# Attention inside a fused layer: products with v for eight key chunks at a time instead of four, and the four score tiles of such a phase issued one by one

## The chip, the cores and the metric

One core of a Trainium2 chip runs the whole program in one launch. The metric is the device time of one execution in microseconds (us); several executions are timed and the median is quoted. TensorE (PE) multiplies, VectorE (DVE) and ScalarE (ACT) work on its results in PSUM, GpSimd (POOL) works in SBUF, SyncE (SP) issues the transfers. "PEld" is TensorE's loading of weights.

## The reference

Three layers follow one another: attention with 32 heads (4 batches of 8), a gated MLP and a channel MLP. Only the first is touched by the change.

```python
q_pool = q.reshape(B, H, S // factor, factor, D).mean(axis=3)        # S 1152 -> 576
scores = scale * np.matmul(q_pool, k.transpose(0, 1, 3, 2))          # 576 x 1152 a head
scores = scores - np.max(scores, axis=-1, keepdims=True)
attn = np.exp(scores)
attn = attn / (np.sum(attn, axis=-1, keepdims=True) + 1e-09)
return np.matmul(attn, v).astype(np.float32)                         # D = 64
```

## The kernel before

Two heads that lie on partitions 0 to 63 and 64 to 127 are worked on together, so `NP` = 16 pairs `j`. A pair's 576 queries are cut in three jobs `u` of `N` = 192, and the 1152 keys in `KC` = 9 chunks of 128: 48 x 9 = 432 units `(u, c)`. The main loop takes them in 108 groups of `G` = 4; a group is two score tiles of two units each. The program is written in the order in which each engine runs it (no scheduler moves anything), so the text of the loop is the order in every engine's queue.

Four kinds of TensorE work alternate in the loop:

- **Scores** (`scores`, L245) and the subtraction of the maximum (`less`, L261 and L264): contraction over 64 rows, two heads side by side in the array. The rows of the trace say 64\*128. ACT then takes the exponential of the whole tile (`expo`, L268) into an SBUF tile `pt` (8 of them), and POOL adds the tiles of a job up for the softmax sum (L282, L285).
- **Pieces** (`piece`): the maxima of the scores are needed before the scores themselves, so rounded copies of q and k are multiplied ahead of time, for a later pair, piece by piece: mostly two matmuls of 512 columns in the 64\*128 form (L161, reduced by DVE at L180), some of 128 columns (L161 with L188, reduced at L191 and after), and 16 in all that use the full array (`c == 2`, L175, rows 128\*128, reduced at L176). `some()` issues one as long as the piece count is behind `end`.
- **Products with v** (`pv`, L292), and the sums over the keys (`sums`, L307): contraction over 128 rows, 64 columns of output a head. The rows say 128\*64. `sums` runs once a job, and ACT copies its result (L311).
- **Transposes** (`to_rows`, L219 and L226), once a pair: they turn the maxima into rows, which ACT copies into `toprow` (L229, L236); `less` needs that.

Score tiles, pieces and transposes share one PSUM ring, the pool `ps_s` with the tag "s" and three slots. The fourth tile to be issued waits until the first one has been read, by ACT if it was a score tile and by DVE if it was a piece.

One group is issued as: a piece; both score tiles; both subtractions and exponentials; a piece; then `pv` for the group before. `also(i)` closes it: it advances the second layer's weight loading by one tick (`Weights.tick`). From group 8 on a unit of weights is begun at every fourth tick, at groups 8, 12, 16 and so on, with two ACT steps in the first tick (L547, L548; the five units of the spatial weights skip them), and one more (L568) six ticks later; DVE steps (L552, L554, L558) lie at ticks one, two and five. In the groups 3 and 4 of a pair, `round_k` (L143) and `round_q` (L132, L137) round the next-but-one pair's k and q on ACT.

Of the kernel before, what the change touches and what calls it, by code (L numbers as in the profile page):

```python
# [31 lines left out]
def attention(tc, idf, q, k, v, xs, rounded, also):  # L32
# [31 lines left out]
    with ExitStack() as ctx, ExitStack() as sco:  # L64
# [84 lines left out]

        pieces = []  # L150
        for u in range(2 * NP):
            for c in range(2):
                pieces += [(u, c, PW * i) for i in range(NPC)]
            pieces += [(u, 2, None)] * (u % 2) + [(u, None, NPC * PW)]
        upto = [sum(x[0] < u for x in pieces) for u in range(2 * NP + 1)]
        done = [0]

# [2 lines left out]
            p = slice(D * e, D * e + D)  # L160
            nc.tensor.matmul(o, s["qr"][p, q0:q0 + 128], s["kr"][p, k0:k0 + n], start=True, stop=True)  # L161

        def piece(r=None):
            u, c, k0 = pieces[done[0]]
            done[0] += 1
            s, jb = st[u // 2], halves[u]
            r = ring("r") if r is None else r
            if "m" not in jb:
                jb["m"] = ld.tile([128, 2, 2, NPC + 1], F32, tag="m", name="m", bufs=4)
                if u % 2:  # L170
                    jb["md"] = ld.tile([128, 2], F32, tag="md", name="md", bufs=2)
            m = jb["m"]
            if c == 2:
                for h in range(NPC):
                    nc.tensor.matmul(r[:, h], s["qd"], s["kr"][:, PW * h:PW * h + PW], start=True, stop=True)  # L175
                nc.vector.tensor_reduce(out=jb["md"][:, 0:1], in_=r, axis=AX.XY, op=ALU.max, negate=True)  # L176
            elif c is not None:
                for e in range(2):
                    rounded_scores(r[:, e], u, c, e, k0, PW)
                nc.vector.tensor_reduce(out=m[:, c, :, k0 // PW], in_=r, axis=AX.X, op=ALU.max, negate=True)  # L180
            else:
                for c in range(2):
                    for e in range(2):
                        rounded_scores(r[:, e, REST * c:REST * c + REST], u, c, e, k0, REST)
                if u % 2:
                    for e in range(2):
                        p = slice(D * e, D * e + D)
                        nc.tensor.matmul(  # L188
                            r[:, e, 2 * REST:3 * REST], s["qd"][p], s["kr"][p, k0:S], start=True, stop=True
                        )  # L190
                nc.vector.tensor_reduce(  # L191
                    out=m[:, :, :, NPC].rearrange("p c e -> p e c"),
                    in_=r[:, :, 0:2 * REST].rearrange("p e (c x) -> p e c x", c=2),
                    axis=AX.X, op=ALU.max, negate=True,
                )
                t = tops[u // 2 % 2]
                if u % 2:
                    for e in range(2):
                        p = slice(D * e, D * e + D)
                        nc.vector.tensor_reduce(  # L200
                            out=jb["md"][p, 1:2], in_=r[p, e, 2 * REST:3 * REST], axis=AX.X, op=ALU.max, negate=True
                        )
                        nc.vector.tensor_reduce(out=t[p, 4, e, 0:1], in_=jb["md"][p], axis=AX.X, op=ALU.min)
                nc.vector.tensor_reduce(
                    out=t[:, 2 * (u % 2):2 * (u % 2) + 2, :, 0], in_=m, axis=AX.X, op=ALU.min
                )
# [31 lines left out]
        def scores(pair):  # L238

            t = ps_s.tile([128, 2, 512], F32, tag="s", name="s")  # L240
            for x, (u, c) in enumerate(pair):
                s, q0 = st[u // 3], N * (u % 3)
                for e in range(2):
                    p = slice(D * e, D * e + D)
                    nc.tensor.matmul(  # L245
                        t[:, e, N * x:N * x + N], s["k"][p, 128 * c:128 * c + 128], s["q"][p, q0:q0 + N],
                        start=x == 0, stop=False,
                    )
            return t
# [37 lines left out]
        def pv(u, c):  # L287
            jb = jobs[u]
            if c == 0:
                jb["o"] = ps_o.tile([128, 512], F32, tag="o", name="po")  # L290
            for e in range(2):
                nc.tensor.matmul(  # L292
                    jb["o"][D * e:D * e + D, 0:N], st[u // 3]["v"][:, e, c], jb["p", c][:, e],
                    start=c == 0, stop=c == KC - 1,
                )

        def sums(u):

            jb = jobs[u]
            terms = [jb["acc"][:, :, N * i:N * i + N] for i in range(W)]  # L300
            terms += [jb["p", c] for c in ((KC - 1,) if u % 2 == 0 else ())]
            if u == NJ - 1:
                terms += [jb["p", c] for c in range(KC - 4, KC)]
            r = jb["o"][:, 256:256 + N]
            for i, x in enumerate(terms):
                for e in range(2):
                    nc.tensor.matmul(  # L307
                        r[D * e:D * e + D], ones, x[:, e], start=i == 0, stop=i == len(terms) - 1
                    )
            t = jb["sum"] = ld2.tile([128, N], F32, tag="sum", name="sum")  # L310
            nc.scalar.activation(t, r, ACTF.Copy, bias=1e-9)  # L311

        def recip(u, i):
            t = jobs[u]["sum"][:, N * i // 2:N * (i + 1) // 2]
            nc.vector.reciprocal(out=t, in_=t)  # L315

        def out(u):
            jb = jobs[u]
            q0 = N * (u % 3)
            x = ld2.tile([128, N], F32, tag="x", name="x")  # L320
            nc.vector.tensor_tensor(out=x, in0=jb["o"][:, 0:N], in1=jb["sum"], op=ALU.mult)
            b, h = divmod(u // 3, HP)
            nc.sync.dma_start(out=xs[b][2 * D * h:2 * D * h + 2 * D, q0:q0 + N], in_=x)
# [18 lines left out]
        pool_q(0, nc.gpsimd, 256, T)  # L342
        round_q(0, 256, T)
        for i in range(upto[1]):
            piece()
            busy(4 if i > 1 else 0)
        pool_q(1, nc.gpsimd)
        busy(14)
# [12 lines left out]
        for i, group in enumerate(groups):  # L361
            for u, c in group:
                if c == KC - 1 and u < NJ - 1:
                    sums_at[i + 1] = u
                    for n in range(2):
                        smalls.setdefault((i + 2, n), []).append(lambda u=u, n=n: recip(u, n))
                    smalls.setdefault((i + 3, 0), []).append(lambda u=u: out(u))
        j = 0
        for i, group in enumerate(groups):
            if j + 1 < NP and at[j + 1] == i:  # L370
                j += 1
            r = i - at[j]
            if r == 0:
                if j + 2 < NP:
                    load_k(j + 2)
                    load_q(j + 2)
                if j + 1 < NP:
                    load_v(j + 1)

            end = min(upto[2] + -(-upto[2] * (4 * i + 8) // (3 * KC)), upto[2 * NP])  # L380

            def some(t=None):
                if done[0] < end:
                    piece(t)

            new = []
            if i == 2:
                new = [1]
            elif r == 0 and j:
                new = [2 * j, 2 * j + 1]  # L390
            for u in new:
                while done[0] < upto[u + 1]:
                    piece()
            if new:
                to_rows(*new)
            else:
                some()
            for x in smalls.pop((i, 0), ()):
                x()
            tiles = [group[x:x + W] for x in range(0, G, W)]  # L400
            ts = [scores(pair) for pair in tiles]
            for pair, t in zip(tiles, ts):
                less(pair, t)
                expo(pair, t)
            some()

            for _ in range(2 if i < 4 else 0):
                if done[0] < end:
                    piece()
            for x in smalls.pop((i, 1), ()):  # L410
                x()
            if i + 1 == len(groups):
                break
            for x in before:
                pv(*x)
            before = group

            if i in sums_at:
                sums(sums_at[i])
            also(i)  # L420
            if r == 2 and j + 2 < NP:
                pool_q(j + 2, nc.gpsimd)

            if r == 3 and j + 2 < NP:
                round_k(j + 2)
            if r == 4 and j + 2 < NP:
                round_q(j + 2)
        sco.close()
        for x in before:
            pv(*x)  # L430
        before = group
        for x, names in zip(before, LEFT):
            pv(*x)
# [832 lines left out]
```

## Time and profile before

| what | us |
|---|---|
| three timed executions: lowest, median, highest | 1159.83, 1162.37, 1163.08 |
| the profiled execution | 1156.86 |
| its span in the trace | 1155.1 |
| mean granted TensorE clock in it | 0.995 of full speed |
| busy: PE, PEld | 1124.0 (97%), 963.8 (83%) |
| busy: DVE, POOL, ACT | 581.3 (50%), 517.4 (45%), 441.8 (38%) |

The profiled execution takes 1.8 us beyond its span, and 5.5 us less than the median. A matmul's end in the trace is modelled and it overlaps the next one's start, so a busy PE says little; what counts is the distance from one start to the next. A float32 matmul shows up as two records, and the two heads run side by side, so "x16" on the score line of a group is eight steps: two tiles of four.

### The profile page before, as it was taken

The numbers are of one execution on the slowest core, as the hardware profiler recorded it, in microseconds if no ns is written. First come the engines' busy times: TensorE is split into PE (matmuls) and PEld (weight loads), VectorE is DVE, ScalarE is ACT, GpSimd is POOL, SyncE is SP. The second block draws the span as 40 slices with busy tenths as digits, with TensorE's granted clock in tenths as the row PEclk, the third lists the DMA queues.
The fourth block names the chain that finished last, engine by engine and source line by source line (L and its number), as shares of the span: only waits on it lengthen the run. The fifth ranks groups of instructions, "written<-read, shape, count | busy, mean of one in ns | idle before, by whom it ended". The sixth has DMA issues, their size and how long they took to land.

```text
span 1155.1 us, 20475 instructions
## 1 busy us (share of the span) xinstructions
PE 1124.0 (97%) x8530; PEld 963.8 (83%) x8530; DVE 581.3 (50%) x882; ACT 441.8 (38%) x822; POOL 517.4 (45%) x400
## 2 busy tenths in 40 slices
PE   7999999999999999999999998999999999999998
PEld 6777777888878888788988997789989999999997
DVE  5667777766778766244242427788722121121211
ACT  3455554555555554443333325455411111111110
POOL 3578786877777776524242427575600000000000
PEclk9999999999999999999999998999999999999999
DMA  6143422333524321011111016244302010010000
GB/s 164 45 122 92 122 79 77 83 99 86 129 76 130 83 73 35 9 57 46 42 42 51 1 51 228 78 146 131 116 1 82 1 35 21 1 55 1 28 1 28
DMA packets 40079, 79.32 MB, mean 69 GB/s; under 512 B 5809, under 2 KB 20145, under 8 KB 39986
## 3 DMA queue, kind: packets, MB, share of 16 engines
q1 hardware_dynamic: 39986, 78.01, 23.0%
q8 instruction: 67, 1.10, 0.4%
q14 instruction: 26, 0.21, 0.1%
HBM read 63.31 MB, written 14.16 MB: 67 GB/s over the span
## 4 chain that ended last, share of the span: by engine, by line
PE 52%; DVE 3%; POOL 1%; ACT 1%; issue 1%; POOLq 0%
PE ph L1114 17%; PE py L1128 17%; PE pu L866 4%; PE pv L731 4%; PE pg L884 4%; PE py L914 3%; DVE st L558 1%; PE pV L939 1%; DVE st L552 1%; PE pt L1106 1%; POOL st L556 1%; PE pU L900 1%; DVE st L554 0%; POOL gt L449 0%; PE po L307 0%
## 5 line engine op out<-in xcount | busy, mean ns | idle before, releaser
L1128 PE MATMUL py<-w,h 128*128 128x512 f32 x864 | 218.4, 397 | 3.0 <-ACT h L1117 2.7
L268 ACT ACTIVATE pt<-s 128x768 f32<-128x768 f32 x216 | 163.3, 808 | 149.8 <-PE s L261 138.8
L1114 PE MATMUL ph<-ut,w 128*128 128x384 f32 x1152 | 218.6, 338 | 0.0
L1114 PEld LDWEIGHTS ph<-ut,w 128*128 128x128 f32 x1152 | 205.7, 188 | 8.5
L180 DVE TENSOR_REDUCE m<-r 128x2 f32<-128x1024 f32 x128 | 155.8, 1223 | 75.4 <-PE r L161 74.9
L282 POOL TENSOR_TENSOR acc<-pt,acc 128x768 f32<-128x768 f32 x94 | 173.4, 1845 | 41.8 <-ACT pt L268 37.4
L1128 PEld LDWEIGHTS py<-w,h 128*128 128x128 f32 x864 | 160.2, 188 | 34.2 <-ACT h L1117 3.3
L1118 DVE SCALAR_TENSOR_TENSOR h<-ph,h 128x384 fp32r<-128x384 f32 x96 | 53.4, 557 | 268.6 <-ACT h L1117 268.6
L292 PE MATMUL po<-pt,v 128*64 128x192 f32 x1728 | 164.5, 332 | 0.0
L245 PE MATMUL s<-q,k 64*128 64x192 f32 x1728 | 163.0, 328 | 1.0 <-ACT pt L268 0.6
L1117 ACT ACTIVATE h<-ph 128x384 fp32r<-128x384 f32 x96 | 47.1, 491 | 304.5 <-PE ph L1114 304.5
L245 PEld LDWEIGHTS s<-q,k 64*128 64x128 f32 x1728 | 142.1, 187 | 11.2 <-issue 4.1
L292 PEld LDWEIGHTS po<-pt,v 128*64 128x64 f32 x1728 | 114.3, 136 | 39.3 <-issue 26.1
L282 POOL TENSOR_TENSOR acc<-pt 128x768 f32<-128x768 f32 x48 | 88.0, 1834 | 83.0 <-ACT pt L268 82.9
L315 DVE RECIPROCAL sum<-sum 128x96 f32<-128x96 f32 x96 | 69.7, 737 | 42.6 <-ACT sum L311 42.6
L161 PE MATMUL r<-yh 64*128 64x512 f32 (+1 forms) x384 | 71.7, 398 | 13.0 <-DVE m L180 7.1
L556 POOL TENSOR_TENSOR st<-st,raw 128x512 int32<-128x512 int32 (+3 forms) x48 | 68.8, 1435 | 19.4 <-issue 11.0
L261 PE MATMUL s<-toprow,yh 64*128 64x384 f32 x416 | 68.2, 401 | 0.0
L161 PEld LDWEIGHTS r<-yh 64*128 64x128 f32 x384 | 34.1, 184 | 40.5 <-issue 12.2
L884 PE MATMUL pg<-wst,vn 128*128 128x288 f32 x448 | 60.1, 295 | 0.0
L884 PEld LDWEIGHTS pg<-wst,vn 128*128 128x128 f32 x448 | 59.6, 188 | 0.0
L866 PEld LDWEIGHTS pu<-xt,wi 128*128 128x128 f32 x384 | 53.3, 188 | 2.1
(125 smaller groups left out, 1291.5 us busy)
## 6 DMA issues: line engine op xcount, KB each, us to landing
raw<-in_moe_w_ch_dram SPq DMA_DIRECT2D x32, 512.0 KB, 3.7
k<-in_k_dram SPq DMA_DIRECT2D x32, 288.0 KB, 4.4
qraw<-in_q_dram SPq DMA_DIRECT2D x32, 288.0 KB, 5.7
v<-in_v_dram SPq DMA_DIRECT2D x16, 576.0 KB, 4.1
x<-x SPq DMA_DIRECT2D x48, 96.0 KB, 1.7
xn<-x SPq DMA_DIRECT2D x4, 1152.0 KB, 5.7
out_dram<-un SPq DMA_DIRECT2D x18, 256.0 KB, 2.1
raw<-in_moe_w_in_dram SPq DMA_DIRECT2D x8, 512.0 KB, 4.3
```

The lines of the kernel that those rows point to most:

```text
L161: nc.tensor.matmul(o, s["qr"][p, q0:q0 + 128], s["kr"][p, k0:k0 + n], start=True, stop=True)
L180: nc.vector.tensor_reduce(out=m[:, c, :, k0 // PW], in_=r, axis=AX.X, op=ALU.max, negate=True)
L245: nc.tensor.matmul(t[:, e, N * x:N * x + N], s["k"][p, 128 * c:128 * c + 128], s["q"][p, q0:q0 + N], start=x == 0, stop=False,)
L268: nc.scalar.activation(x, t[:, :, 0:W * N], ACTF.Exp, scale=SC)
L282: nc.gpsimd.tensor_tensor(out=a, in0=x, in1=jb["t"] if c < 4 else a, op=ALU.add)
L292: nc.tensor.matmul(jb["o"][D * e:D * e + D, 0:N], st[u // 3]["v"][:, e, c], jb["p", c][:, e], start=c == 0, stop=c == KC - 1,)
L315: nc.vector.reciprocal(out=t, in_=t)
L556: nc.gpsimd.tensor_tensor(out=o, in0=o, in1=lo, op=ALU.add)
L866: nc.tensor.matmul(p[:, 0:HT], wi[0][:, a, k, 128 * m:128 * m + 128], xt[:, c, k, HT * h:HT * h + HT], start=i == 0, stop=i == 3 * KD - 1,)
L884: nc.tensor.matmul(p[:, 0:HT], vn[:, a, s, 128 * m:128 * m + 128], wst[:, c, s, sl], start=s == 0 and i == 0, stop=s == NT - 1 and i == 1,)
L1114: nc.tensor.matmul(p[:, 0:BT], w1s[m][:, a, k], ut[i][:, c, k], start=j == 0, stop=j == 3 * KD - 1)
L1128: nc.tensor.matmul(py[i][c], h[:, a, 128 * c:128 * c + 128], w2s[m][:, e], start=m == 0 and a + e == 0, stop=m == KM - 1 and a == 1,)
```

## The change

`pv` and `sums` run in odd groups alone, for the two groups before: 16 matmul instructions instead of 8 (a phase is an even group and the odd one behind it). A score tile's subtraction and exponential follow it at once, before the next tile's scores. Pieces go to the front of the even group, to its end, and to the end of the odd group, where there can be two; full-array pieces are swapped with the next one unless they lie beside the products with v. The sums, reciprocals and outputs of a job move with `pv`. The names "r0" and "r1" take slots of the same ring.

```diff
@@ -149,9 +149,10 @@
 
         pieces = []
         for u in range(2 * NP):
+            pieces += [(u, 2, None)] * (u % 2)
             for c in range(2):
                 pieces += [(u, c, PW * i) for i in range(NPC)]
-            pieces += [(u, 2, None)] * (u % 2) + [(u, None, NPC * PW)]
+            pieces += [(u, None, NPC * PW)]
         upto = [sum(x[0] < u for x in pieces) for u in range(2 * NP + 1)]
         done = [0]
 
@@ -160,8 +161,11 @@
             p = slice(D * e, D * e + D)
             nc.tensor.matmul(o, s["qr"][p, q0:q0 + 128], s["kr"][p, k0:k0 + n], start=True, stop=True)
 
-        def piece(r=None):
-            u, c, k0 = pieces[done[0]]
+        def piece(r=None, beside=True):
+            x = done[0]
+            if not beside and pieces[x][1] == 2 and pieces[x + 1][1] is not None:
+                pieces[x], pieces[x + 1] = pieces[x + 1], pieces[x]
+            u, c, k0 = pieces[x]
             done[0] += 1
             s, jb = st[u // 2], halves[u]
             r = ring("r") if r is None else r
@@ -342,7 +346,7 @@
         pool_q(0, nc.gpsimd, 256, T)
         round_q(0, 256, T)
         for i in range(upto[1]):
-            piece()
+            piece(ps_s.tile([128, 2, 512], F32, tag="s", name="r0") if i % 3 else None)
             busy(4 if i > 1 else 0)
         pool_q(1, nc.gpsimd)
         busy(14)
@@ -361,10 +365,11 @@
         for i, group in enumerate(groups):
             for u, c in group:
                 if c == KC - 1 and u < NJ - 1:
-                    sums_at[i + 1] = u
+                    at_sum = i + 1 + i % 2
+                    sums_at.setdefault(at_sum, []).append(u)
                     for n in range(2):
-                        smalls.setdefault((i + 2, n), []).append(lambda u=u, n=n: recip(u, n))
-                    smalls.setdefault((i + 3, 0), []).append(lambda u=u: out(u))
+                        smalls.setdefault((at_sum + 1, n), []).append(lambda u=u, n=n: recip(u, n))
+                    smalls.setdefault((at_sum + 2, 0), []).append(lambda u=u: out(u))
         j = 0
         for i, group in enumerate(groups):
             if j + 1 < NP and at[j + 1] == i:
@@ -379,9 +384,9 @@
 
             end = min(upto[2] + -(-upto[2] * (4 * i + 8) // (3 * KC)), upto[2 * NP])
 
-            def some(t=None):
-                if done[0] < end:
-                    piece(t)
+            def some(beside=False, lag=0):
+                if done[0] < end - lag:
+                    piece(beside=beside)
 
             new = []
             if i == 2:
@@ -393,30 +398,33 @@
                     piece()
             if new:
                 to_rows(*new)
-            else:
-                some()
+            elif i % 2 == 0:
+                some(True)
             for x in smalls.pop((i, 0), ()):
                 x()
-            tiles = [group[x:x + W] for x in range(0, G, W)]
-            ts = [scores(pair) for pair in tiles]
-            for pair, t in zip(tiles, ts):
+            for x in range(0, G, W):
+                pair = group[x:x + W]
+                t = scores(pair)
                 less(pair, t)
                 expo(pair, t)
-            some()
+            some(bool(i % 2))
+            if i % 2 and i > 3:
+                some(True)
 
             for _ in range(2 if i < 4 else 0):
                 if done[0] < end:
-                    piece()
+                    piece(ps_s.tile([128, 2, 512], F32, tag="s", name="r1"))
             for x in smalls.pop((i, 1), ()):
                 x()
             if i + 1 == len(groups):
                 break
-            for x in before:
-                pv(*x)
-            before = group
-
-            if i in sums_at:
-                sums(sums_at[i])
+            if i % 2:
+                for x in before:
+                    pv(*x)
+                before = []
+                for u in sums_at.pop(i, ()):
+                    sums(u)
+            before = before + group
             also(i)
             if r == 2 and j + 2 < NP:
                 pool_q(j + 2, nc.gpsimd)
@@ -428,6 +436,10 @@
         sco.close()
         for x in before:
             pv(*x)
+        for i in sorted(sums_at):
+            for u in sums_at[i]:
+                if u < NJ - 1:
+                    sums(u)
         before = group
         for x, names in zip(before, LEFT):
             pv(*x)
```

How the engines' rows move. First TensorE in groups 8 and 9: `r` is a piece, `s` a score tile, `po` the output of `pv`. Before:

```order
L161 MATMUL r<-yh 128x128 x4
L245 MATMUL s<-q,k 128x192 x8
L261 MATMUL s<-toprow,yh 128x384 x4
L161 MATMUL r<-yh 128x512 x2
L292 MATMUL po<-pt,v 64x192 x8
L161 MATMUL r<-yh 128x512 x2
L245 MATMUL s<-q,k 128x192 x8
L261 MATMUL s<-toprow,yh 128x384 x4
L292 MATMUL po<-pt,v 64x192 x8
```

The same two groups with the change (the lines are numbered four higher there):

```order
L249 MATMUL s<-q,k 128x192 x4
L265 MATMUL s<-toprow,yh 128x384 x2
L249 MATMUL s<-q,k 128x192 x4
L265 MATMUL s<-toprow,yh 128x384 x2
L162 MATMUL r<-yh 128x128 x4
L249 MATMUL s<-q,k 128x192 x4
L265 MATMUL s<-toprow,yh 128x384 x2
L249 MATMUL s<-q,k 128x192 x4
L265 MATMUL s<-toprow,yh 128x384 x2
L179 MATMUL r<-yh 128x512 x2
L162 MATMUL r<-yh 128x512 x2
L296 MATMUL po<-pt,v 64x192 x16
```

The four score tiles now stand between one pair of `pv` blocks, and the second block is gone. From the first score row to the last, the array form changes 229 times before and 128 times with the change; blocks of `pv` and `sums` are left 106 and 53 times.

Second, the waits of TensorE on its ring, in group 37 before (two score tiles, a piece, `pv`); a bracket names the engine whose progress an instruction waits for:

```order
L161 MATMUL r<-yh 128x512 [waits DVE_49]
L161 MATMUL r<-yh 128x512
L245 MATMUL s<-q,k 128x192 [waits Activation_49]
L245 MATMUL s<-q,k 128x192 x3
L245 MATMUL s<-q,k 128x192 [waits Activation_49]
L245 MATMUL s<-q,k 128x192 x3
L261 MATMUL s<-toprow,yh 128x384 x4
L161 MATMUL r<-yh 128x512 [waits DVE_49]
L161 MATMUL r<-yh 128x512
L292 MATMUL po<-pt,v 64x192 x8
```

And the second half of the same phase with the change, from the third score tile on:

```order
L249 MATMUL s<-q,k 128x192 [waits DVE_49]
L249 MATMUL s<-q,k 128x192 x3
L265 MATMUL s<-toprow,yh 128x384 x2
L249 MATMUL s<-q,k 128x192 [waits Activation_49]
L249 MATMUL s<-q,k 128x192 x3
L265 MATMUL s<-toprow,yh 128x384 x2
L162 MATMUL r<-yh 128x512 [waits Activation_49]
L162 MATMUL r<-yh 128x512
L162 MATMUL r<-yh 128x512 [waits Activation_49]
L162 MATMUL r<-yh 128x512
L296 MATMUL po<-pt,v 64x192 x8
```

The last piece now takes the slot of the third score tile and waits for that tile's exponential; `pv` stands behind it in the queue. No `pv` lies between the tile and the piece any more.

Third, ACT in the groups 36 and 37, with `pt` the exponentials, `st` and `raw` the weight steps, `yh<-k` and `yh<-q` the roundings. Before (the first row holds group 35, too):

```order
L268 ACTIVATE pt<-s 128x768 x4
L311 ACTIVATE sum<-po 128x192
L547 ACTIVATE st_101<-raw_96 128x512
L548 ACTIVATE raw_96<-raw_96 128x512
L143 CAST yh<-k 128x1152
L268 ACTIVATE pt<-s 128x768 x2
L132 CAST yh<-q 128x512
L137 CAST yh<-q 64x64 x2
```

With the change:

```order
L272 ACTIVATE pt<-s 128x768 x2
L559 ACTIVATE st_101<-raw_96 128x512
L560 ACTIVATE raw_96<-raw_96 128x512
L143 CAST yh<-k 128x1152
L272 ACTIVATE pt<-s 128x768 x2
L315 ACTIVATE sum<-po 128x192
L132 CAST yh<-q 128x512
L137 CAST yh<-q 64x64 x2
```

The weight steps and the rounding keep their place between the exponentials of group 36 and those of group 37. On TensorE a block of `pv` lay beside that place before; with the change it lies in the middle of the four score tiles.

## Rows read from the trace of the kernel before

**Rows 1.** Windows, groups' stretch: length, busy us (count) by engine, PEclk, DMA share, GB/s.

```profile
50.00:485.00 435.00, 425.77 (x4654) 344.94 (x4654) 298.25 (x422) 232.66 (x399) 330.07 (x210) 1.00 0.32 89
```

**Rows 2.** Source line of the scores: duration ns min/median/max, first and last start.

```profile
L245 PE MATMUL s<-q,k x1728: 320/322/427, 18.1 to 484.7; 64*128 64x192 f32 x192
```

**Rows 3.** Timeline of PE, 200 to 225: start us, us, engine, line, operation, form.

```profile
203.83 1.52 PE L292 MATMUL po<-pt,v 128*64 128x192 f32 x16
205.28 0.50 PE L161 MATMUL r<-yh 64*128 64x512 f32 x2
205.62 1.47 PE L245 MATMUL s<-q,k 64*128 64x192 f32 x16
206.78 0.65 PE L261 MATMUL s<-toprow,yh 64*128 64x384 f32 x4
207.26 0.40 PE L161 MATMUL r<-yh 64*128 64x512 f32 x2
207.59 1.52 PE L292 MATMUL po<-pt,v 128*64 128x192 f32 x16
208.94 0.82 PE L307 MATMUL po<-acc,ones 128*64 128x192 f32 x8
209.69 0.44 PE L161 MATMUL r<-yh 64*128 64x128 f32 x4
...
219.81 0.65 PE L261 MATMUL s<-toprow,yh 64*128 64x384 f32 x4
220.38 1.52 PE L292 MATMUL po<-pt,v 128*64 128x192 f32 x16
```

**Rows 4.** Waits, 45 to 500: engine line waited for: us in total, times, longest.

```profile
ACT pt L268 <- PE s L261: 129.1, 86, 3.7
...
PEld po L292 <- issue: 25.3, 91, 0.4
...
PE r L161 <- DVE m L180: 6.8, 8, 2.4
```

**Rows 5.** Timeline of all engines, 205.2 to 214; in brackets the idle time before, and its releaser.

```profile
207.35 1.51 ACT L268 ACTIVATE pt<-s 128x768 f32<-128x768 f32 x2 [2.25 <-PE s L261]
```

**Rows 6.** Groups of ACT by form, 50 to 485: busy us, mean ns, idle before.

```profile
L268 ACT ACTIVATE pt<-s 128x768 f32<-128x768 f32 x202 | 152.7, 808 | 137.6 <-PE s L261 126.5 <-PE s L264 3.0 <-POOL acc L282 2.3
...
L229 ACT CAST toprow<-tr 128x512 fp32r<-128x512 f32 x15 | 8.8, 584 | 6.9 <-PE tr L226 6.9
...
L236 ACT CAST toprow<-tr 64x64 fp32r<-64x64 f32 x30 | 6.2, 206 | 0.2
L568 ACT CAST wi<-st 128x512 fp32r<-128x512 f32 x8 | 4.9, 616 | 0.1
```

**Rows 7.** Timeline of all engines, 175 to 200.

```profile
174.53 1.21 DVE L180 TENSOR_REDUCE m<-r 128x2 f32<-128x1024 f32 x1
...
175.79 0.19 PEld L161 LDWEIGHTS r<-yh 64*128 64x128 f32 x2 [1.11 <-DVE m L180]
...
186.98 0.67 ACT L547 ACTIVATE st<-raw 128x512 f32<-128x512 f32 x1
...
187.55 0.66 ACT L548 ACTIVATE raw<-raw 128x512 int32<-128x512 uint32 x1
...
188.11 1.14 ACT L143 CAST yh<-k 128x1152 fp32r<-128x1152 f32 x1
...
189.15 1.50 ACT L268 ACTIVATE pt<-s 128x768 f32<-128x768 f32 x2
...
190.55 0.62 ACT L132 CAST yh<-q 128x512 fp32r<-128x512 f32 x1
...
191.06 0.50 ACT L137 CAST yh<-q 64x64 fp32r<-64x64 f32 x2
191.13 4.10 POOL L282 TENSOR_TENSOR acc<-pt,acc 128x768 f32<-128x768 f32 x2
191.26 2.30 DVE L558 SCALAR_TENSOR_TENSOR st<-raw,st 128x512 int32<-128x512 int32 x1
```

## The prediction, written before the changed kernel ran

> **What bounds the kernel now.** I read the windows first. Over 50 to 485 us, which is nearly all of the attention loop, PE is busy for 425.77 of 435 us at the full granted clock, POOL for 330, DVE for 298 and ACT for 233 [rows 1]; the loop's scores run from 18.1 to 484.7 us [rows 2]. So TensorE sets the pace here, and a microsecond that its queue loses or gains moves everything behind it. The second view is PE's timeline, read from start to start, since ends are modelled [rows 3]. It gives these steps:
>
> - A step of `pv` or `sums`: eight of `pv` take 208.94 - 207.59 = 1.35 when `sums` follows, four of `sums` 0.75 when a piece follows. With 0.10 for the change of form (next line) off, a step is 0.65 / 4 = 0.1625, and the first of a block costs 1.35 - 1.30 = 0.05 extra.
> - Leaving the 128\*64 form: `pv` to a piece is 205.28 - 203.83 = 1.45, against 1.35: 0.10.
> - Leaving the 64\*128 form: `less` to `pv` is 0.57, `less` to a piece 0.48: 0.09.
> - A piece: 0.34 behind `pv`, and 0.33 ahead of `pv`, of which 0.09 is the leaving: 0.24 by itself, so entering 64\*128 costs 0.10.
> - A group's scores and subtractions: 207.26 - 205.62 = 1.64, so 0.82 a tile, of which `less` is 0.17.
>
> A round trip between the two forms thus costs 0.05 + 0.10 + 0.09 + 0.10 = 0.34. The third view is the waits [rows 4]: the loading of `pv`'s weights stood still 91 times for 25.3 us with no releaser, 0.28 each time, which is the same cost seen at the weight loads. The only ring wait of size is a piece that waits for DVE, 6.8 us in 8 cases. ACT waits for TensorE for 129.1 us: it has slack now, and no score tile of the loop is held up by it for long.
>
> **The change, part by part.**
>
> *Fewer changes of form.* Of 106 blocks of `pv` and `sums` 53 are left: 53 x 0.34 = 18.0 us less. All form changes fall from 229 to 128, five less than these 106 would make, since full-array pieces now lie more often between pieces: 5 x 0.10 = 0.5 back. I take -17.5. The bounds: the two drains alone are 53 x 0.19 = -10; two gaps of 0.28 at the weight loads would be 53 x 0.56 = -30. I stay with the start-to-start figure, since the path is made of starts. The Trainium skill states in "TensorEngine Tiling (Array Packing)", Key Properties, that changing the tiling mode drains TensorE. The trace agrees with 0.09 and 0.10 for the two drains; the page gives no price.
>
> *Tiles one by one.* Scores (float32) and `less` (rounded) alternate twice as often. 107 groups at 1.64 - 8 x 0.1625 - 2 x 0.17 = 0.00 extra: nothing, at most 0.02 x 107 = 2. PE's own order covers it.
>
> *The ring in the middle of a phase.* This is the new wait. Count from the start of the first tile's scores. A tile is through TensorE every 0.82. Its exponential starts 0.26 after that: in rows 5 it starts at 207.35, 1.73 after the scores' start, and the first tile was through one `less` ahead of 1.64, at 1.47 [rows 3, 5]. It lasts 0.81 [rows 6], two take 1.51 so the second starts 0.70 after the first, and a waiting weight load follows a reader by 0.05 (174.53 + 1.21 to 175.79) [rows 7]. So a slot comes back 0.26 + 0.81 + 0.05 = 1.12 after its tile is through. Before, `pv` (1.35) lay in that time. Now:
>
> - The third tile wants the first one's slot, and between lie the second tile and a piece, 0.82 + 0.24 = 1.06. It is 0.06 late, and with its weights not loaded ahead (an estimate from the 0.05 of `pv`'s first step) 0.11. 32 phases have that piece: 3.5 us.
> - The last piece wants the third tile's slot; between lie the fourth tile and a piece, again 1.06: 0.11 late. But ACT's queue holds the weight steps and roundings between the second and the third exponential (the third place in the order). ACT is free for them at 1.64 + 0.26 + 0.70 = 2.60, and the third exponential could start at 1.64 + 0.24 + 0.11 + 0.82 + 0.26 = 3.07: 0.47 is hidden, the rest delays the last piece, and `pv` and the sums queue behind it. Without the middle piece only 0.12 is hidden.
> - From start to start [rows 7] the two weight steps take 188.11 - 186.98 = 1.13, `round_k` 1.04, `round_q` 0.51 + 0.50; L568 takes 0.616 less 0.10 of overlap, 0.52 [rows 6].
> - In the order with the change, of the phases that end in two pieces: 10 have at most L568 there and lose 1.6 in all; groups 20, 60 and 72 (1.13, middle piece) lose 0.77 each, 2.3; 4 and 10 (`round_q`) 0.65 each, 1.3; 64 (2.14) 1.8; without the middle piece 36 (2.17) loses 2.2, 44 (1.01) 1.0, 50 (1.56) 1.55, 58 (1.53) 1.5, 90 (1.46) 1.45; 8, 28 and 88, where a long full-array piece gives cover or the weights are small, 1.6 together. Sum 16.3. Phases with a transpose in the middle have its own time as cover and are left out.
> - `less` of a pair's first tile waits for `toprow`: 0.26 + 0.48 + 2 x 0.21 + 0.05 = 1.21 [rows 6] against 0.65 of one tile's scores, where two tiles' were in between. 0.56 in the 7 places where a new pair's first tile opens a group: 3.9.
>
> Together 3.5 + 16.3 + 3.9 = +23.7. It could be 12 if the slots came back 0.2 sooner than I have them, and 36 if each of the roughly 65 late slots cost 0.15 more.
>
> *DVE's stall.* Before, a piece waits for the last piece's reduction where a weight step of 2.30 (which ran beside POOL) stood in DVE's queue [rows 4, 7]. From the first closing piece to the next phase's second, TensorE now does 0.24 + 0.33 + 2.65 + about 0.5 of sums + 0.34 + 1.64 = 5.7, and DVE three reductions of 1.21 and weight steps of up to 3, 6.6; the late piece above hides about as much. Most of the 6.8 goes; I take -5.5, bounds 0 and -6.8.
>
> *What costs nothing.* The added `pt` tiles in use (six of eight) fit, since a tile's slot comes up again two phases on. ACT's work of odd groups lies under 2.65 us of `pv`. The sums come later, and POOL has that time. The later layers keep their order. If `pv` were not there as cover, ACT's 1 us in odd groups would show as in the even ones.
>
> The sum: -17.5 + 23.7 - 5.5 = +0.7, less than a measurement of this kernel can tell from no change (0.3%, 3.5 us). On the profiled 1156.86 that is 1157.6; it stood 5.5 under the median of 1162.37, so on the median 1163.1. As the lateness of 0.06 is at the edge of what modelled ends allow, and slots that come back 0.06 sooner would take some 4 us off the sum, I put the forecast a little lower, at 1162.
>
> **The rivals.**
>
> *Faster.* The slots come back in time and only the long ACT steps show, at two thirds of what I have: -17.5 - 5.5 + 11 = -12, so 1150; with next to no stall it is 1140. For it: ACT is busy for 233 of 435 us [rows 1]. Against it: the waits are latencies, not loads, and the order names them.
>
> *Slower: the readers of PSUM set the phase.* Three or four pieces now fall in two clumps around one `pv` block. If DVE is late with the first piece of a phase by its weight step, its reciprocals and the two closing reductions together, the middle piece waits as well, in each of 50 phases. Beyond 5.7 us of DVE work between the closing pieces and that one, each costs its excess; 0.5 us in half of them is 12, and no DVE stall goes away: +20, so 1182 at the end, 1175 at half the place. For it: DVE has 298 us of work in 435 [rows 1]. Against it: 5.7 us holds most of it. The Trainium skill speaks for this one in "TensorEngine Tiling (Array Packing)", PSUM Bottleneck: tiling makes TensorE faster but not the emptying of PSUM. The trace bears it out in the 8 waits for DVE alone.
>
> *The drains are not saved*, because the time of a round trip was in truth weight loading, which comes back elsewhere: then -10 in place of -17.5, and +10 altogether, 1172.
>
> **Chances.** The forecast, between 1154 and 1170, has 0.50; within it 0.26 lie within 0.3% of the old time, 0.13 below, 0.11 above. Faster has 0.26, the readers as bound 0.16, the drains not saved 0.08. That makes 0.39 faster, 0.26 the same, 0.35 slower. The range leaves out 0.1 at each end: 1146 to 1175.
>
> **What would show it.** `pv`'s weight loads should stand still about 50 times, not 91, with the same 0.28 each. TensorE should show new waits for ACT (`r` or `s` on `pt`), 15 to 25 us in the loop, longest around 2 us near the groups 36 and 64, and those for DVE should shrink below 3. The last score should start within 4 us of 484.7. If the waits for ACT come to less than 10 us, I am wrong towards faster; if those for DVE grow, or POOL's `acc` holds up `sums`, towards slower.

## The result, and the profile after

The changed kernel took 1168.32 us in the median (1166.48 to 1169.63, 6 runs), the one before 1161.94 beside it; the ratio is 1.0067 (95% interval 1.0053 to 1.0081), 0.5 to 0.8% slower. "No change", forecast at 1162, was wrong, though the range of 1146 to 1175 held the time. The profiled execution took 1169.63, its span 1167.9.

First the line of the scores, by source line as in [rows 2]:

```profile
L249 PE MATMUL s<-q,k x1728: 320/322/428, 20.3 to 494.9; 64*128 64x192 f32 x192
```

The loop runs for 474.6 us instead of 466.6. Its start is 2.2 later in this execution, whose mean granted clock is 0.85 over the first 17 us (1.00 before; the best kernel below starts at 17.9, also at 1.00). From its last score to the end of the span go 673.0 us instead of 670.4; 2.3 of these are work that the change moves behind the loop, four more units of `pv` and the sums of one more job (fourteen steps of 0.1625). So the loss is in the loop, and with that work counted it is some 10 us there; the medians differ by 6.4, since the profiled execution before was 5 us under its median. The waits of the changed kernel from 45 to 510 us, columns as in [rows 4]:

```profile
ACT pt L272 <- PE s L265: 50.4, 44, 4.1
...
PE r L162 <- ACT pt L272: 17.8, 16, 5.3
PEld po L296 <- issue: 12.3, 44, 0.4
...
ACT st L559 <- DMA raw<-in_moe_w_in_dram: 5.1, 1, 5.1
...
PE r L162 <- DVE m L184: 1.1, 2, 0.6
...
PE s L265 <- ACT toprow L233: 0.9, 2, 0.7
```

`pv`'s weight loads stand still 44 times for 12.3 us, not 91 times for 25.3, and the wait for DVE has gone from 6.8 to 1.1. In their place TensorE waits for ACT, 17.8 us in 16 cases, and ACT waits less for TensorE (50.4 instead of 129.1): the slack moved. Two of the cases in the timeline, first the groups 36 and 37, where the order showed the longest queue:

```profile
189.65 1.63 ACT L272 ACTIVATE pt<-s 128x768 f32<-128x768 f32 x2 [0.93 <-PE s L265]
...
191.18 0.67 ACT L559 ACTIVATE st<-raw 128x512 f32<-128x512 f32 x1
...
191.75 0.65 ACT L560 ACTIVATE raw<-raw 128x512 int32<-128x512 uint32 x1
191.86 0.40 PE L162 MATMUL r<-yh 64*128 64x512 f32 x2
...
192.29 1.14 ACT L143 CAST yh<-k 128x1152 fp32r<-128x1152 f32 x1
...
193.33 1.51 ACT L272 ACTIVATE pt<-s 128x768 f32<-128x768 f32 x2
194.20 0.19 PEld L162 LDWEIGHTS r<-yh 64*128 64x128 f32 x2 [2.32 <-ACT pt L272]
194.20 0.50 PE L162 MATMUL r<-yh 64*128 64x512 f32 x2 [1.94 <-ACT pt L272]
...
194.63 2.82 PE L296 MATMUL po<-pt,v 128*64 128x192 f32 x32
```

The third exponential waits behind three other steps of its own engine until 193.33; the last piece, which needs that tile's slot, idles for 1.94 us, and `pv`, whose operands were long there, begins behind it at 194.63. Second, the groups 8 and 9:

```profile
62.65 0.72 PE L179 MATMUL r<-yh 128*128 128x512 f32 x2
...
66.71 0.66 ACT L559 ACTIVATE st<-raw 128x512 f32<-128x512 f32 x1 [5.14 <-DMA raw<-in_moe_w_in_dram]
67.27 0.64 ACT L560 ACTIVATE raw<-raw 128x512 int32<-128x512 uint32 x1
67.81 1.50 ACT L272 ACTIVATE pt<-s 128x768 f32<-128x768 f32 x2
...
68.66 0.79 PE L162 MATMUL r<-yh 64*128 64x512 f32 x2 [5.29 <-ACT pt L272]
```

The same place, but ACT itself stands for 5.14 us: its first weight step waits for a transfer. TensorE idles for 5.29.

### The profile page after: what moved, and what is told of

Read it like the earlier page. It is cut to its first block, busy times and chain, and to the rows that moved or that the text cites. A ratio compares the mean times of both kernels' runs of the same rounds, so it can differ in the third digit from the quotient of the medians.

```text
span 1167.9 us, 20472 instructions
## 1 busy us (share of the span) xinstructions
PE 1124.2 (96%) x8530; PEld 973.5 (83%) x8530; DVE 583.5 (50%) x882; ACT 447.7 (38%) x822; POOL 517.7 (44%) x400
## 4 chain that ended last, share of the span: by engine, by line
PE 52%; DVE 3%; POOL 1%; issue 1%; ACT 1%; POOLq 0%
PE ph L1126 17%; PE py L1140 16%; PE pu L878 4%; PE pv L743 4%; PE pg L896 4%; PE py L926 4%; DVE st L570 1%; PE pV L951 1%; PE pt L1118 1%; POOL st L568 1%; PE pU L912 1%; DVE st L564 1%; POOL gt L461 0%; DVE st L566 0%; PE po L311 0%
## 5 line engine op out<-in xcount | busy, mean ns | idle before, releaser
L272 ACT ACTIVATE pt<-s 128x768 f32<-128x768 f32 x216 | 171.6, 810 | 59.8 <-PE s L265 54.6
L249 PE MATMUL s<-q,k 64*128 64x192 f32 x1728 | 183.0, 330 | 0.7
L296 PE MATMUL po<-pt,v 128*64 128x192 f32 x1728 | 155.5, 332 | 0.9 <-DVE x L325 0.9
L296 PEld LDWEIGHTS po<-pt,v 128*64 128x64 f32 x1728 | 120.0, 138 | 30.1 <-issue 12.7
L265 PE MATMUL s<-toprow,yh 64*128 64x384 f32 x416 | 98.9, 468 | 0.9 <-ACT toprow L233 0.9
L162 PE MATMUL r<-yh 64*128 64x512 f32 (+1 forms) x384 | 70.3, 396 | 22.2 <-ACT pt L272 18.6
L315 ACT ACTIVATE sum<-po 128x192 f32<-128x192 f32 x48 | 15.9, 330 | 162.0 <-PE po L311 127.8
```

Source lines behind the costliest of these rows:

```text
L249: nc.tensor.matmul(t[:, e, N * x:N * x + N], s["k"][p, 128 * c:128 * c + 128], s["q"][p, q0:q0 + N], start=x == 0, stop=False,)
L265: nc.tensor.matmul(t[:, e, 0:2 * N], first[p], m, start=False, stop=True)
L272: nc.scalar.activation(x, t[:, :, 0:W * N], ACTF.Exp, scale=SC)
L296: nc.tensor.matmul(jb["o"][D * e:D * e + D, 0:N], st[u // 3]["v"][:, e, c], jb["p", c][:, e], start=c == 0, stop=c == KC - 1,)
```

## The experiments

Theory A: what stands in ACT's queue between the second and the third exponential of a phase holds up the last piece and all behind it, the late transfer included. Theory B: those steps are innocent; the form changes were never worth 17.5 us, and the loss is in weight loads that are not made ahead.

**ACT's steps to the odd groups** (`ticks_odd`):

```diff
+            if i % 2:
+                also(i - 1)
             if i + 1 == len(groups):
                 break
...
-            also(i)
+            if i % 2:
+                also(i)
...
-            if r == 3 and j + 2 < NP:
+            odd = at[j] % 2
+            if r == 3 - odd and j + 2 < NP:
                 round_k(j + 2)
-            if r == 4 and j + 2 < NP:
+            if r == 3 + odd and j + 2 < NP:
                 round_q(j + 2)
```

> The changed kernel, but the second layer's weight steps and the roundings of k and q, which ran between the second and the third exponential of a phase, run in odd groups alone, behind the fourth exponential and ahead of the products with v. Theory A (ACT's steps in the middle of a phase hold up the last piece and all behind it): the waits of pieces for ACT, 19.6 us in the loop, fall below 5, and the time falls by 12 to 16 us against the changed kernel, to 1153 to 1157. Theory B (those steps are innocent; the loss is in weight loads that are not made ahead and in form changes that were never worth much): the time stays within 4 us of 1168.

Measured 1152.8 (1151.42 to 1153.47), ratio to before 0.9933 (0.9918 to 0.9948): 15.5 us faster than the changed kernel. In its waits one piece is left that waits for ACT, 0.2 us (the changed kernel has 18.6 us of such waits from 45 us on and 19.4 in the whole loop, where the expectation says 19.6), but some score tiles now wait:

```profile
PE s L249 <- ACT pt L272: 5.1, 6, 1.5
ACT st L563 <- DMA raw<-in_moe_w_in_dram: 4.3, 1, 4.3
PE r L162 <- DVE m L184: 2.4, 2, 1.3
PE r L162 <- ACT pt L272: 0.2, 1, 0.2
```

Theory A stands; B, which had the time within 4 us of 1168, falls, though its doubt of the 17.5 us comes out right below. ACT still waits 4.3 us for the transfer, now beside `pv`; behind it TensorE idles for 1.30 us (for DVE, whose own queue waited for that weight step) and for 1.47 us (for a slot).

**The transfer earlier** (`early_load`):

```diff
-        if i == WEIGHTS:
+        if i == WEIGHTS - 3:
             w.load(units, raws)
```

> The changed kernel with one edit: the first transfers of the second layer's weights are issued at group 5 instead of group 8. Theory A: the one wait of a piece of 5.3 us in group 9, where ACT stood 5.1 us for such a transfer with the third exponential behind it, goes, and nothing else: 1163 to 1165. Theory B: that wait belongs to the profiled execution alone and the time stays at 1168.

Measured 1161.63 (11 runs), ratio 1.0010 (1.0001 to 1.0019): 6.7 us less from this line alone, more than expected. In the loop it is 5.6 (474.6 to 469.0). The rest was not taken apart; the mean granted clocks of these executions are 0.991 to 0.994, those of the changed kernel 0.987 to 0.991. Its waits:

```profile
PE r L162 <- ACT pt L272: 12.3, 15, 1.9
```

One case fewer, and 5.5 us less; the longest is now the 1.9 of group 37. The wait was thus no accident of the profiled execution.

**The same edit on the kernel before** (`before_early_load`):

> The kernel before, with the first transfers of the second layer's weights issued at group 5 instead of 8 (the edit of early_load). Theory A: before the change ACT's 3.5 us of waiting for that transfer lay under products with v, so nothing moves: 1157 to 1162, within 0.2% of before. Rival (the transfer's lateness costs either kernel): 4 to 6 us faster than before.

Measured 1160.18, ratio 1.0002 (0.9989 to 1.0016): nothing, though there too ACT stood for the transfer. These are the row of the kernel before, from the view of [rows 4], and the only idle time of TensorE behind it, in the timeline:

```profile
ACT st L547 <- DMA raw<-in_moe_w_in_dram: 3.5, 1, 3.5
```

```profile
67.21 1.61 PE L245 MATMUL s<-q,k 64*128 64x192 f32 x16 [0.63 <-ACT pt L268]
```

The lateness was always there, and `pv` covered all but 0.63 us of it. The change took this cover away.

**Both edits** (`ticks_odd_early`):

> Both edits together. Theory A: the late transfer is partly hidden already when ACT's steps lie ahead of the products with v, so the sum of both gains is not reached: 1151 to 1156. Theory B: 1163 to 1168.

Measured 1149.77 (1147.27 to 1149.93), ratio 0.9900 (0.9882 to 0.9918): another 3.0 on `ticks_odd`, less than the 6.7 alone, as theory A has it. The time itself lies below the 1151 to 1156 that it named.

**Two tiles together again** (`two_tiles`):

```diff
-            for x in range(0, G, W):
-                pair = group[x:x + W]
-                t = scores(pair)
-                less(pair, t)
+            tiles = [group[x:x + W] for x in range(0, G, W)]
+            ts = [scores(pair) for pair in tiles]
+            for pair, t in zip(tiles, ts):
+                less(pair, t)
                 expo(pair, t)
```

> The changed kernel with the two score tiles of a group issued as before: both scored, then both subtracted and exponentiated. Theory A (slots that come back late set the phase): the first exponential starts 0.65 us later, and so do the third tile and the last piece in most of the phases with pieces between: 15 to 30 us slower, 1183 to 1198. Theory B: the ring has room, the time stays within 4 us of 1168.

Measured 1204.44, ratio 1.0378 (1.0361 to 1.0395): 36 us slower than the changed kernel, more than the 15 to 30.

```profile
PE r L162 <- ACT pt L272: 24.2, 28, 4.6
PE s L249 <- ACT pt L272: 17.0, 32, 0.6
```

Score tiles now wait 32 times, about half a microsecond each: an exponential that starts one tile's scores (0.65) later returns its slot that much later. With four tiles between blocks of `pv`, one by one is what makes the phase bearable.

**One by one in the kernel before** (`before_one_by_one`, the reverse edit on the old loop):

> The kernel before with one edit: the two score tiles of a group scored, subtracted and exponentiated one after the other. Theory A: products with v lie between a group's tiles and the next claim on their slots, so nothing is won by an earlier exponential, and alternating the two kinds of matmul costs at most 2 us: 1159 to 1164. Rival: the alternation itself costs 0.05 us or more a tile: 1166 or more.

Measured 1160.75 beside 1158.36, ratio 1.0012 (0.9996 to 1.0028): not told from no change, as theory A expects; the rival's 1166 is outside.

**A round trip by itself** (`no_pieces_four` and `no_pieces_eight`). The main lines, in both:

```diff
-            end = min(upto[2] + -(-upto[2] * (4 * i + 8) // (3 * KC)), upto[2 * NP])
+            end = min(upto[2] + -(-upto[2] * (4 * i + 8) // (3 * KC)), upto[2])
...
-                new = [2 * j, 2 * j + 1]
+                st[j]["top"] = st[0]["top"]
...
-                top, q0 = st[u // 3]["top"], N * (u % 3)
+                top, q0 = st[0]["top"], N * (u % 3)
...
-            if r == 3 and j + 2 < NP:
-                round_k(j + 2)
...
-            if r == 4 and j + 2 < NP:
-                round_q(j + 2)
```

> The kernel before without the pieces and the roundings of all pairs but the first (the first pair's maxima are subtracted everywhere, so the output is not the attention's): score tiles and products with v alone, four chunks at a time. To be set against no_pieces_eight, which has the same work in the changed order. Theory F and theory S both put a round trip without pieces at 0.24 us (0.05 into pv, 0.10 out, 0.09 out of the scores), so this one is the slower of the two by 53 x 0.24 = 13 us, less what late slots cost the other. Rival (only leaving pv costs something): 5 us.

> The changed kernel without the pieces and the roundings of all pairs but the first (same change of the output as in no_pieces_four). With no piece behind the third tile, nothing queues behind ACT's steps in the middle of a phase until the next phase, so theory A expects no wait of TensorE for ACT over 2 us in sum. Faster than no_pieces_four by 13 us (theories F and S), by 5 us (the rival).

Measured 1098.62 (1097.92 to 1098.98) and 1084.04 (1083.26 to 1084.46): 14.6 us apart, a little over the 13 and far from the rival's 5. These whole times are no clean price of 53 round trips. All four executions of the second kernel had a lower granted clock (0.987 to 0.989, against 0.992 to 0.995; in the profiled ones 0.89 against 1.00 over the first 30 us, with scores that start 2.1 later), and 2.3 us of `pv` and `sums` move behind its loop. From the first score to the last the loops take 406.07 and 387.14 us: 18.9 less, 16.7 without the moved work, 0.31 a round trip. Their waits, in the same order, 30 to 430 us:

```profile
PEld po L292 <- issue: 24.9, 101, 0.3
PE po L307 <- POOL acc L282: 7.1, 7, 1.5
```

```profile
PEld po L296 <- issue: 12.6, 52, 0.4
...
PE po L311 <- POOL acc L286: 7.3, 5, 2.7
```

Half the stand-stills of weight loads go, the wait for POOL is nearly the same, and TensorE does not wait for ACT in the second one: the difference in the loop is form changes. The timelines of PE give the price from start to start, a group of the first kernel and a phase of the second:

```profile
208.18 1.52 PE L292 MATMUL po<-pt,v 128*64 128x192 f32 x16
209.63 1.57 PE L245 MATMUL s<-q,k 64*128 64x192 f32 x16
210.90 0.65 PE L261 MATMUL s<-toprow,yh 64*128 64x384 f32 x4
211.48 1.52 PE L292 MATMUL po<-pt,v 128*64 128x192 f32 x16
```

```profile
208.09 2.82 PE L296 MATMUL po<-pt,v 128*64 128x192 f32 x32
210.74 0.82 PE L311 MATMUL po<-acc,ones 128*64 128x192 f32 x8
211.49 0.92 PE L249 MATMUL s<-q,k 64*128 64x192 f32 x8
212.11 0.47 PE L265 MATMUL s<-toprow,yh 64*128 64x384 f32 x2
212.42 0.81 PE L249 MATMUL s<-q,k 64*128 64x192 f32 x8
...
214.58 0.47 PE L265 MATMUL s<-toprow,yh 64*128 64x384 f32 x2
214.99 2.82 PE L296 MATMUL po<-pt,v 128*64 128x192 f32 x32
```

A group takes 211.48 - 208.18 = 3.30, and a phase 214.99 - 208.09 = 6.90, of which four steps of `sums` are 0.65. So 2 x 3.30 - 6.25 = 0.35 is a round trip between score tiles. Both theories had 0.24: they left out what entering the 64\*128 form costs a score tile, 0.10 (212.11 - 211.49 = 0.62 from its scores to its `less`, against 0.52 for a tile behind another).

**Blocks of eight put back** (`eight_by_group`):

```diff
-                    at_sum = i + 1 + i % 2
+                    at_sum = i + 1
...
-            if i % 2:
-                for x in before:
-                    pv(*x)
-                before = []
-                for u in sums_at.pop(i, ()):
-                    sums(u)
-            before = before + group
+            for x in before:
+                pv(*x)
+            for u in sums_at.pop(i, ()):
+                sums(u)
+            before = group
```

> The kernel of ticks_odd_early with the products with v (and the sums) issued in every group for the group before, eight matmul instructions at a time, as before the change; tiles one by one, pieces and ACT's steps stay where they were. It puts back the 53 round trips between the two array forms. Theory F (a round trip costs the 0.34 us of the prediction): +18 us against 1149.8, less up to 7 us of waits of TensorE for ACT that go: 1161 to 1168. Theory S (a piece costs its 0.33 us wherever it stands, so that a round trip costs 0.10 to 0.19): +5 to +10 less up to 7: 1148 to 1153.

Measured 1169.73 beside 1158.36, ratio 1.0089 (1.0063 to 1.0115), against 0.9900: 1.9%, some 22 us, more than either theory had. It is no clean price of a round trip, since DVE's waits came back:

```profile
PE r L162 <- DVE m L184: 8.7, 8, 2.7
```

**And with two tiles together** (`eight_two_tiles`, the edit of `two_tiles` on it):

> The kernel of eight_by_group with a group's two tiles scored together and then subtracted together, as before the change: the kernel before, but for the places of the pieces, ACT's steps and the early load. If alternating scores and subtractions costs about 0.04 us a group (before_one_by_one suggests 2 to 4 us in all), this is 2 to 6 us faster than eight_by_group, 1163 to 1168. Rival: with two pieces in a row ahead of pv the later exponentials hold up the ring even here, and it is slower than eight_by_group, by 5 us or more.

Measured 1190.3, ratio 1.0254 (1.0233 to 1.0274): the rival, slower by some 19 us. Its pieces wait for exponentials:

```profile
PE r L162 <- ACT pt L272: 15.2, 27, 0.9
```

In `eight_by_group` this was 1.1 us in one case. The second of the two pieces that close an odd group takes the slot of that group's own first tile, and when the two tiles are issued together its exponential starts later. What is left of the change here is mainly where the pieces stand, next to the places of ACT's steps and the early load. That the places of the pieces make up the 31 us against the kernel before was not tested by themselves, but the parts of the change clearly need one another.

**The rounding ahead of `pv`** (`rounding_ahead`). The trace of `ticks_odd_early` has six waits of score tiles for ACT where both roundings stood behind the copy of the sums, four of about 0.95 us and two of 0.36 (the expectation counts five of 0.95), so `round_k` goes in front:

```diff
             if i % 2:
                 also(i - 1)
+            odd = at[j] % 2
+            if r == 3 - odd and j + 2 < NP:
+                round_k(j + 2)
             if i + 1 == len(groups):
                 break
...
-            odd = at[j] % 2
-            if r == 3 - odd and j + 2 < NP:
-                round_k(j + 2)
             if r == 3 + odd and j + 2 < NP:
```

> The kernel of ticks_odd_early with the rounding of k moved from behind the sums' copy on ACT to ahead of the products with v. Five waits of about 0.95 us of the third or second tile for ACT follow groups in which both roundings stand between the sums' copy and the next exponential. Theory A: they shrink to nothing, 3 to 5 us faster than ticks_odd_early: 1144 to 1147. Rival: the rounding then delays the fourth exponential's reader or the sums' copy instead, 1149 to 1152.

Measured 1142.63 (1141.37 to 1143.01), ratio 0.9847 (0.9831 to 0.9862): 1.5% faster than before, the fastest here, and 7.1 us less than `ticks_odd_early` (6.3 in the loop), more than the 3 to 5 expected. Of the waits of TensorE for DVE and ACT in the loop one line over 0.2 us is left, and its scores end at 466.4:

```profile
PE r L162 <- DVE m L184: 1.3, 2, 1.1
```

```profile
L249 PE MATMUL s<-q,k x1728: 320/322/428, 17.9 to 466.4; 64*128 64x192 f32 x192
```

## Why the prediction was wrong

**The step that failed** is in "the ring in the middle of a phase": I put ACT's steps there at their durations and not at what they themselves wait for. The phase of group 8 is one of three that stand in my sum at 1.6 us together; its last piece alone idled for 5.29. The first weight step waits for its transfer, in the kernel before, too (3.5 us, a row of the waits that I had and left out), and with the change that wait lies on the path. With the transfer early the loop is 5.6 us and the median 6.7 us shorter, which is about all of the 6.4 by which the kernel became slower: the ratio is then 1.0010, +1.2 us, where the sum said +0.7. That these two lie so close is luck: the gain from form changes, the largest term, was too large by some 6 to 10 us, while the long queues, `toprow` and DVE's stall came out better than in the sum, by some 6 to 8 us together (all below). The forecast below the sum, at 1162, went the wrong way too: the slots did not come back sooner. The third tile behind a piece is late by what the sum has for it: in 29 of 32 phases it takes 0.62 us from its scores to its `less` (210.95 - 210.33 in the lines below) instead of 0.52 (209.72 - 209.20).

**The long queues** were right in place and nearly in size. In the trace of the changed kernel the idle time before the last piece is 1.94 us in group 37 (2.2 with its weights), 1.53 in 65 (1.8), 1.41 in 51 (1.55), 1.34 in 59 (1.5), 1.17 in 91 (1.45), 0.83 in 45 (1.0), 0.49 to 0.63 in 21, 61 and 73 (0.77), 0.40 in 5 and 11 (0.65); the forecast, which counts 0.11 of lateness with the weights more, is in brackets. Moving what stands there took 15.5 us off.

**Form changes** were too dear in my sum at 17.5. The 0.34 of a round trip holds between score tiles (0.35 in the pair without pieces), but not between pieces. In the changed kernel's timeline of PE a piece between two tiles takes 210.33 - 210.03 = 0.30, one behind `pv` 0.34, and one ahead of `pv` was 0.33 [rows 3]:

```profile
209.20 0.81 PE L249 MATMUL s<-q,k 64*128 64x192 f32 x8
209.72 0.47 PE L265 MATMUL s<-toprow,yh 64*128 64x384 f32 x2
210.03 0.40 PE L162 MATMUL r<-yh 64*128 64x512 f32 x2
210.33 0.92 PE L249 MATMUL s<-q,k 64*128 64x192 f32 x8
210.95 0.47 PE L265 MATMUL s<-toprow,yh 64*128 64x384 f32 x2
```

So a piece pays 0.04 for entering the form and 0.03 for leaving it, and a round trip between pieces is 0.05 + 0.10 + 0.03 + 0.04 = 0.22, or 11.7 us for 53. Before the change 77 of the 106 blocks stood behind a piece and 83 ahead of one. The 0.24 that I had for a bare piece was never seen; it came from a piece ahead of `pv`, less the 0.09 that a score tile pays there.

**DVE's stall**: 6.8 to 1.1, so -5.7 against -5.5, and a wait of 1.8 us behind a full-array piece (L176) went as well. **`toprow`**: 0.9 us in 2 waits of PE, and 0.4 in 2 more at L268, against 3.9 in 7 places; why the others did not wait was not taken apart. **Alternating** was taken as nothing; `before_one_by_one` can't tell +0.12% from it. Four sums beside the forecast do not come out as printed, and decide nothing: by their own figures the bounds 12 and 36 are 10.7 and 33.5, and the rivals' +20 and +10 are +18.2 and +8.2.

**Together**: from [rows 2] to `rounding_ahead` the loop falls from 466.6 to 448.5, by 18.1. Added up from start to start, 10.1 of it are rows of `pv` and `sums`: 2.3 moved behind the loop, and 7.8 for 53 blocks, the 0.15 of each. Another 8.8 is idle time of TensorE, DVE's stall above all (12.1 to 3.3). All other rows together are 0.8 longer, 3.0 of late third tiles included, so form changes gave some 10 us in all. The changed kernel's loop is 26.1 us longer than that of `rounding_ahead`; 20.1 of this is idle time of TensorE (23.4 against 3.3), 5.6 of it the late transfer (`early_load` ends its scores at 487.0 from 18.0, 469.0). The gain was real, and ACT's queue ate it.

The rival "the readers of PSUM set the phase" came closest, with the wrong reader: I had DVE, and it was ACT. The Trainium skill's sentence in "TensorEngine Tiling (Array Packing)", PSUM Bottleneck, that tiling does not speed up the emptying of PSUM, fits what `two_tiles` shows, where emptying 0.65 us later costs 36 us; by ACT's load alone (233 of 435 us busy) it would not have shown, since it is a latency. The rival "the drains are not saved" was nearest in time, and its -10 is about what form changes gave, but not for its reason: the drains of `pv` were saved, and a piece beside `pv` pays less for the form than a score tile does.

Open: why `eight_by_group` is 11 us slower than the kernel before although it has the old blocks. Its trace shows one part: 49 of its blocks are followed at once by score tiles, which pay 0.10 for entering the form, and 7 before. At 0.06 more than a piece pays that is an estimate of 2.5 us. Places of pieces and ACT's steps were not taken apart there.

## What to carry to other kernels

When work is batched to change an engine's mode less often, list what the removed block covered: here each `pv` between two groups hid not only the exponentials but whatever else stood in ACT's queue, nearly all of a late transfer included. For every instruction that moves off cover, price its own waits, not only its duration. Then move the other work of that queue under the block that is left: two small moves of ACT's steps and one earlier transfer turned +0.67% into -1.5%.

## What was not expected of the hardware

Two float32 score tiles and their rounded subtractions cost TensorE nothing measurable more when alternated (1.0012, 0.9996 to 1.0028), while the same order decides 3% (1.0067 against 1.0378) through the ring. And a piece of 512 columns takes 0.30 us between two score tiles, not the 0.24 that the rows ahead of `pv` suggested, so that a round trip to the 128\*64 form and back costs 0.35 us between score tiles and 0.22 between pieces.
